# The shifted word of a float64 decoder moves from SBUF into idle columns of the attention's score banks, and h, y and the transposed tails share three PSUM buffers

## The chip, the cores and the metric

The program runs on one core of one Trainium2 chip. Its time is device microseconds from launch to end. The engines are named as in the profile: PE (TensorE, the matrix engine), PEld (its weight loads), DVE (VectorE), ACT (ScalarE), POOL (GpSimd) and SP (SyncE, which issues DMAs). Two kernels are held to differ when their times differ by more than about 0.2%.

## The reference, cut to what matters

Eight batches of eight heads, 576 positions, 64 columns per head; then a two-layer feed-forward network over all 4608 positions.

```python
scores = scale * q @ k.T                          # (8, 8, 576, 576)
thresh = max(scores, -1) - tau
scores = where(scores >= thresh, scores, -1e9)
attn = softmax(scores)
x = (attn @ v), heads side by side                # (4608, 512)
h = x @ w_in                                      # (512, 2048), w_in is float64
out = (h * tanh(softplus(h))) @ w_out             # (2048, 512), w_out is float64
```

The two weight matrices arrive as float64. The kernel turns them into float32 itself, from the two 32-bit words of each number: this is the decoding that the change edits.

## The kernel before

**Attention, and the first layer in its shadow.** The work is cut into 288 steps g. A step handles 128 query rows of a pair of heads; nine steps make a pair, 36 a batch. The scores of step g lie in one of two PSUM tiles, `s0` and `s1`, taken in turn (`smap[g % 2]`). Such a tile is two whole banks, 2 x 512 float32 columns a partition; the scores take 290 columns of the first bank and 286 of the second, a few columns at 508 hold a constant, and the rest is unused. In step g DVE takes the row maximum (`row_max`, "TENSOR_REDUCE st<-s" in the profile), ACT the exponential ("ACTIVATE e<-s,st"), DVE the mask with the row sum (`masked`, "SCALAR_TENSOR_TENSOR p<-s,st,e"), POOL the normalisation ("TENSOR_SCALAR p<-p,st"). One step later and more PE transposes p (tile `tp` for four blocks, `t5` for the tail block, shown as "t" in the profile, since numbers are left out of names), ACT rounds the transposed block to `hi`, DVE makes the rest `lo` (and `tk` for the tails), and PE multiplies them with v into `y`. From step 42 on PE also runs the first layer of the batch before (`gemm1`, matmuls into `h`), handed out in portions of a few matmuls per step (table `MIX`). ACT copies each finished h to `hst`, which goes to DRAM.

**Where the scores are issued.** `begin(g + 1)` issues the scores of the next step on PE. Up to step 41 it stands at the start of step g. From `LATE = 42` on it stands at the end of step g, in the middle of that step's portion of h matmuls. In both places it reuses the bank pair that step g - 1 read last, so its first matmul waits for `masked(g - 1)` on DVE.

**Decoding.** A piece is 128 x 256 numbers. ACT scales both words (`first`), DVE clamps the upper one from columns `a` to `b` (`clamp`, TENSOR_SCALAR on float32), shifts it from `b` back into `a` (`shift`, TENSOR_SCALAR on uint32), and merges the sign bit (`sign`, SCALAR_TENSOR_TENSOR on uint32, which reads `b` and `a`); POOL adds the lower word (`add`). All of it lies in SBUF (tile `dec`). There are 32 pieces of w_in, decoded in steps 3 to 55, then 16 pieces of half of w_out (`decode_w2`), one every 14 steps, and 16 pieces more that are decoded near the end of attention or later. For w_in, shift and sign follow each other in one step (`STAGES`, the first two entries); for `decode_w2` the sign comes two steps after the shift. In a step the shift is issued before `masked(g)`; the sign is issued before it up to step 38 and behind it from `JOIN = 39` on.

**PSUM.** There are eight banks. While attention runs: two for h and y in turn (pool `psh`), four for the scores, one for `tp`, one for `t5`. In the last batch's first layer, when attention is over, the banks of scores, tp and t5 have gone; three of h's five buffers are then in another pool (`psx`, "hx" in the profile), three are for the second layer.

**The second layer** follows, from about 980 us on: seven products per pair of token blocks (tiles x, y, z) over blocks of g = mish(h) read back from DRAM.

**What sets the order.** On PE, DVE, ACT and POOL the instructions run exactly in the order in which the Python code emits them (`InOrder`); each engine stops at the first instruction whose wait is not met. Waits are put in by the framework: an instruction that writes a tile waits for those that used it before, and a buffer that comes round waits for its last readers.

## Time and profile before

| | |
|---|---|
| median of 3 runs | 1331.6 us (1330.83 to 1331.86) |
| the profiled execution | 1333.22 us, of which the span of instructions is 1331.4 us |
| granted PE clock, mean | 0.997 |
| PE busy | 1296.8 us, 97% |
| PE weight loads | 1257.4 us, 94% |
| DVE busy | 1152.3 us, 87% |
| ACT busy | 1031.8 us, 77% |
| POOL busy | 750.0 us, 56% |

Nearly all instructions carry line 95 (the recording helper), so rows are told apart by operation and tiles. A row of the grouped view reads: line, engine, operation, out<-in, shape, count | busy time in all, mean ns of one | idle time of the engine before them and what ended it. A matmul's end is modelled, so two matmuls that follow each other overlap in the rows; the distance from start to start (about 0.13 us for an h matmul) is the pace. What an instruction of DVE takes contains the time in which it was held up after its start.

### The profile page before, as it was taken

To read this page: it belongs to the slowest core of one execution; us is meant where nothing else is said; L and a number is where in the kernel's file an instruction comes from. 1 tells how busy PE (TensorE), PEld (TensorE's weight loads), DVE (VectorE), ACT (ScalarE), POOL (GpSimd) and SP (SyncE) were. 2 spreads that over 40 slices of the span, in tenths; PEclk is the share of its full clock that TensorE was granted. 3 is DMA by queue.
4 is the path that set the end of the run, shared out by engine and by line. 5 is a ranking of instruction groups with operands and counts; after the bars stand their busy time and mean duration, and the time that the engine had idled before them with its cause. 6 is when DMAs were issued, how large, how long until landed. Compare 5 with 4: busy or idle time off the path is not lost.

```text
span 1331.4 us, 29917 instructions
## 1 busy us (share of the span) xinstructions
PE 1296.8 (97%) x9931; PEld 1257.4 (94%) x9931; DVE 1152.3 (87%) x2941; ACT 1031.8 (77%) x2320; POOL 750.0 (56%) x1080
## 2 busy tenths in 40 slices
PE   8997899999999999999999999999999999999998
PEld 7666889999999999999999999999999999999998
DVE  7999999999999999999999999997978666778764
ACT  6888788888888888888888888877767666557562
POOL 4879888788788887888878788774100000000000
PEclk9999999999999999999999999999999999999999
DMA  5333334333343343333433333324745454554430
GB/s 186 111 101 110 117 118 129 103 114 112 99 135 91 109 125 98 123 104 108 130 94 117 108 113 122 95 68 157 245 138 152 128 132 138 159 151 112 112 118 33
DMA packets 145930, 160.29 MB, mean 120 GB/s; under 512 B 34928, under 2 KB 128112, under 8 KB 145520
## 3 DMA queue, kind: packets, MB, share of 16 engines
q1 hardware_dynamic: 145776, 158.38, 39.1%
q8 instruction: 79, 1.29, 0.4%
q14 instruction: 75, 0.61, 0.2%
HBM read 109.05 MB, written 49.28 MB: 119 GB/s over the span
## 4 chain that ended last, share of the span: by engine, by line
PE 72%; DVE 13%; ACT 10%; issue 4%; POOL 0%; DVEq 0%; ACTq 0%; POOLq 0%
PE h L95 20%; PE y L95 16%; PE x L95 11%; PE s L95 8%; PE z L95 7%; PE tp L95 6%; DVE st L95 5%; ACT e L95 4%; DVE p L95 4%; PE hx L95 2%; DVE dec L95 2%; DVE lo L95 1%; ACT hi L95 1%; DVE tk L95 1%; ACT k L95 1%
## 5 line engine op out<-in xcount | busy, mean ns | idle before, releaser
L95 PE MATMUL h<-xh,w1h 128*128 128x288 f32 x952 | 288.0, 302 | 1.4 <-ACT yo L95 0.7
L95 PE MATMUL h<-xh,w1l 128*128 128x288 f32 x952 | 285.8, 300 | 0.0
L95 POOL TENSOR_SCALAR p<-p,st 128x576 f32<-128x576 f32 x288 | 244.5, 849 | 66.8 <-DVE st L95 44.2
L95 PE MATMUL h<-xl,w1h 128*128 128x288 f32 x952 | 281.3, 295 | 0.3 <-DVE xl L95 0.3
L95 ACT ACTIVATE e<-s,st 128x580 f32<-128x580 f32 x288 | 215.0, 747 | 62.9 <-DVE st L95 55.9
L95 DVE SCALAR_TENSOR_TENSOR p<-s,st,e 128x580 f32<-128x580 f32 x288 | 236.3, 820 | 19.3 <-ACT e L95 8.3
L95 PE MATMUL s<-k,q 128*128 128x286 f32 (+1 forms) x1280 | 231.2, 307 | 10.0 <-DVE p L95 9.6
L95 DVE TENSOR_REDUCE st<-s 128x1 f32<-128x580 f32 x288 | 217.9, 757 | 1.7 <-PE s L95 0.3
L95 PEld LDWEIGHTS s<-k,q 128*128 128x128 f32 x1280 | 189.0, 190 | 23.9 <-DVE p L95 21.0
L95 DVE TENSOR_TENSOR ring<-un,ring 128x512 fp32r<-128x512 f32 x252 | 157.0, 686 | 54.3 <-ACT ring L95 53.9
L95 DVE TENSOR_TENSOR lo<-tp,hi 128x512 fp32r<-128x512 f32 (+1 forms) x280 | 174.0, 630 | 27.6 <-ACT hi L95 23.6
L95 PE MATMUL tp<-ident,p 128*128 128x128 f32 x1152 | 174.1, 274 | 8.6 <-DVE lo L95 6.4
L95 PEld LDWEIGHTS h<-xh,w1h 128*128 128x128 f32 x952 | 179.9, 189 | 2.7 <-ACT yo L95 1.4
L95 ACT CAST hi<-tp 128x512 fp32r<-128x512 f32 (+1 forms) x280 | 149.8, 546 | 39.8 <-PE tp L95 35.3
L95 PEld LDWEIGHTS h<-xl,w1h 128*128 128x128 f32 x952 | 179.5, 189 | 0.5 <-DVE xl L95 0.5
L95 PEld LDWEIGHTS h<-xh,w1l 128*128 128x128 f32 x952 | 179.6, 189 | 0.0
L95 ACT CAST ring<-un 128x512 fp32r<-128x512 f32 x252 | 138.1, 618 | 32.4 <-DVE un L95 32.1
L95 PE MATMUL x<-ring,un 128*128 128x256 f32 x1296 | 156.4, 280 | 0.5 <-ACT ring L95 0.5
L95 PEld LDWEIGHTS tp<-ident,p 128*128 128x128 f32 x1152 | 139.3, 141 | 17.4 <-issue 6.4
L95 PEld LDWEIGHTS x<-ring,un 128*128 128x128 f32 x1296 | 153.9, 189 | 0.6 <-ACT ring L95 0.6
L95 PE MATMUL y<-hi,vs 128*128 128x256 f32 (+1 forms) x448 | 133.3, 320 | 8.0 <-ACT hst L95 6.9
L95 PE MATMUL y<-lo,vs 128*128 128x256 f32 (+1 forms) x448 | 122.7, 296 | 0.0
(78 smaller groups left out, 2537.4 us busy)
## 6 DMA issues: line engine op xcount, KB each, us to landing
hd<-hst SPq DMA_DIRECT2D x56, 576.0 KB, 3.4
r<-q SPq DMA_DIRECT2D x120, 160.0 KB, 2.3
r<-k SPq DMA_DIRECT2D x120, 160.0 KB, 2.3
out_t<-ost SPq DMA_DIRECT2D x36, 256.0 KB, 2.3
r<-v SPq DMA_DIRECT2D x56, 160.0 KB, 2.3
dec<-w_in SPq DMA_DIRECT2D x32, 256.0 KB, 2.9
un<-hd SPq DMA_DIRECT2D x16, 512.0 KB, 5.8
dec<-w_out SPq DMA_DIRECT2D x28, 256.0 KB, 2.8
```

The source lines that it names most:

```text
L95: made = method(*args, **kwargs)
```

## The change

The shifted word is no longer put into columns `a` of the SBUF tile. `shift` writes it as 2 x 128 columns, from column 320 on, into both banks of a score tile: that of the next step, `smap[1 - g % 2]`, with g the step in which the shift is issued (`turn`). `sign` reads it from there, wherever it comes later. This holds for all pieces of w_in, for the 16 of `decode_w2` and for 5 of the rest.

The pool `psh` gets three buffers in place of two, and the tail transposes `t5` take theirs from it, in turn with h and y, in place of a bank of their own. In the last batch's first layer three of five h tiles now come from `psh` and two from `psx`, where it was two and three.

```diff
-    def __init__(self, nc, st, hi, lo, to=None):
+    def __init__(self, nc, st, hi, lo, to=None, bits=None):
...
+        self.bits, self.t, self.tb = bits, self.a, self.b
...
     def shift(self):
-        self.nc.vector.tensor_scalar(self.a, self.b, 3, 0x7FFFFFF8, ALU.logical_shift_left, ALU.bitwise_and)
+        if self.bits:
+            self.t, self.tb = self.bits(), self.b.rearrange("p (a n) -> p a n", a=2)
+        self.nc.vector.tensor_scalar(self.t, self.tb, 3, 0x7FFFFFF8, ALU.logical_shift_left, ALU.bitwise_and)
...
     def sign(self):
-        self.nc.vector.scalar_tensor_tensor(self.b, self.b, 0x80000000, self.a, ALU.bitwise_and, ALU.bitwise_or)
+        self.nc.vector.scalar_tensor_tensor(self.tb, self.tb, 0x80000000, self.t, ALU.bitwise_and, ALU.bitwise_or)
...
-        psh = outer.enter_context(tc.tile_pool(name="psh", bufs=2, space=PSUM))
+        psh = outer.enter_context(tc.tile_pool(name="psh", bufs=3, space=PSUM))
...
-                smap, emap = [], []
+                smap, emap, turn = [], [], [0]
...
+                def bits():
+                    return smap[1 - turn[0] % 2][:, :, 320:320 + WC // 2].bitcast(U32)
...
-                    work = Decode(nc, home(), None, None, r12[:, f % 8])
+                    work = Decode(nc, home(), None, None, r12[:, f % 8], bits if n < 5 else None)
...
-                    work = Decode(nc, st, hi, lo)
+                    work = Decode(nc, st, hi, lo, None, bits)
...
-                    work = Decode(nc, st, None, None)
+                    work = Decode(nc, st, None, None, None, bits)
...
-                        t5 = pst.tile([P, P], F32, name="t5")
+                        t5 = psh.tile([P, P], F32, name="t5", tag="ph")
...
-                            if b < B - 1 or f % 5 < 2:
+                            if b < B - 1 or f % 5 < 3:
...
                 for g in range(NT + 5):
+                    turn[0] = g
...
-            psx = second.enter_context(tc.tile_pool(name="psx", bufs=3, space=PSUM))
+            psx = second.enter_context(tc.tile_pool(name="psx", bufs=2, space=PSUM))
```

The order of instructions on PE, DVE, ACT and POOL stays as it was up to the end of attention. What changes is what the instructions touch. The first place is DVE at the first piece of `decode_w2`, steps 62 to 65. In the rows `s0_121` and `s1_127` are the two score tiles, `dec_3299` the piece, `p` the masked probabilities, `st` small per-row numbers. The shift with its neighbours, before:

```order
L95 TENSOR_TENSOR lo_3527<-tp_3561,hi_3526 128x4x128
L95 TENSOR_TENSOR tk_3528<-t5_3566,tk_3528 64x128 x2
L95 TENSOR_SCALAR dec_3299<-dec_3299 128x256
L95 SCALAR_TENSOR_TENSOR p_3606,st_3582<-s0_121,st_3582,e0_122 128x580
L95 TENSOR_REDUCE st_3630<-s1_127 128x1
```

and of the change:

```order
L95 TENSOR_TENSOR lo_3527<-tp_3561,hi_3526 128x4x128
L95 TENSOR_TENSOR tk_3528<-t5_3566,tk_3528 64x128 x2
L95 TENSOR_SCALAR s1_127<-dec_3299 128x2x128
L95 SCALAR_TENSOR_TENSOR p_3606,st_3582<-s0_121,st_3582,e0_122 128x580
L95 TENSOR_REDUCE st_3630<-s1_127 128x1
```

The shift of step 62 now writes `s1`, which the scores of step 63 write next on PE. The sign, two steps later, before:

```order
L95 TENSOR_TENSOR lo_3627<-tp_3670,hi_3626 128x4x128
L95 TENSOR_TENSOR tk_3628<-t5_3675,tk_3628 64x128 x2
L95 SCALAR_TENSOR_TENSOR p_3709,st_3692<-s0_121,st_3692,e0_122 128x580
L95 SCALAR_TENSOR_TENSOR dec_3299<-dec_3299 128x256
L95 TENSOR_REDUCE st_3743<-s1_127 128x1
```

and of the change:

```order
L95 TENSOR_TENSOR lo_3627<-tp_3670,hi_3626 128x4x128
L95 TENSOR_TENSOR tk_3628<-t5_3675,tk_3628 64x128 x2
L95 SCALAR_TENSOR_TENSOR p_3709,st_3692<-s0_121,st_3692,e0_122 128x580
L95 SCALAR_TENSOR_TENSOR dec_3299<-dec_3299,s1_127 128x256
L95 TENSOR_REDUCE st_3743<-s1_127 128x1
```

The sign of step 64 stands behind that step's mask (`p_3709` from `s0`), reads `s1`, and the next use of `s1` on PE is the scores of step 65. In the built program the first matmul of those scores waits for the count of DVE's semaphore that this sign raises; before, it waited for the count that the mask of step 63 raises. The scores of step 63 wait in the same way for the shift of step 62, where they waited for the mask of step 61.

The second place is PE in step 64, where a tail transpose and a y follow each other (`t5_3675`, `y_3678`), with what they wait for at the end of a row. Before:

```order
L95 MATMUL tp_3670<-ident_80,p_3507 128x128 x3
L95 MATMUL t5_3675<-ident_80,p_3507 128x128
L95 MATMUL y_3678<-hi_3526,vs_3090 128x256 [waits Activation_49]
L95 MATMUL y_3678<-lo_3527,vs_3090 128x256
L95 MATMUL y_3678<-hi_3526,vs_3090 128x256
```

and of the change:

```order
L95 MATMUL t5_3675<-ident_80,p_3507 128x128 [waits Activation_49]
L95 MATMUL y_3678<-hi_3526,vs_3090 128x256 [waits Activation_49]
L95 MATMUL y_3678<-lo_3527,vs_3090 128x256
L95 MATMUL y_3678<-hi_3526,vs_3090 128x256
L95 MATMUL y_3678<-lo_3527,vs_3090 128x256
```

The order of the two is the same. The tail transpose now takes part in the round of h and y, and waits for ACT's copy out of the tile that had its buffer before it.

## The prediction

> **What bounds the kernel now.** I read the table of stages first: for each stretch its length, then busy time of PE, its weight loads, DVE, ACT and POOL, the granted clock and the DMA share.

> ```profile
> 0.00:131.00 131.00, 115.98 (x625) 90.55 (x626) 118.53 (x392) 103.05 (x259) 96.24 (x119) 0.99 0.43 127
> 131.00:190.00 59.00, 52.79 (x371) 50.08 (x371) 56.89 (x167) 46.70 (x120) 50.68 (x64) 0.96 0.41 127
> 190.00:900.00 710.00, 702.64 (x5389) 692.70 (x5388) 660.79 (x1923) 608.61 (x1471) 583.70 (x872) 1.00 0.35 109
> 940.00:1331.40 391.40, 386.41 (x3263) 386.04 (x3261) 283.98 (x382) 244.23 (x394) 1.08 (x1) 1.00 0.46 130
> ```

> There are two regimes. Up to 190 us, while w_in is decoded, DVE bounds (56.89 of 59.00 us between 131 and 190). From 190 on PE bounds: 702.64 of 710.00, so at most 7.4 us of its idle time can be won there, and whatever stops PE for longer comes on top. DVE has 49 us free in that stretch.

> The grouped view gives what the two edited instructions cost, sign (SCALAR_TENSOR_TENSOR) and shift (TENSOR_SCALAR); the two pairs are of 0 to 131 and of 190 to 900 us:

> ```profile
> L95 DVE SCALAR_TENSOR_TENSOR dec<-dec 128x256 uint32<-128x256 uint32 x24 | 17.9, 747 | 0.7
> L95 DVE TENSOR_SCALAR dec<-dec 128x256 uint32<-128x256 uint32 x24 | 8.9, 370 | 0.0
> ...
> L95 DVE SCALAR_TENSOR_TENSOR dec<-dec 128x256 uint32<-128x256 uint32 x16 | 11.3, 706 | 0.0
> L95 DVE TENSOR_SCALAR dec<-dec 128x256 uint32<-128x256 uint32 x16 | 5.9, 369 | 0.2
> ```

> How long they take undisturbed is in the view of the tile dec (minimum/median/maximum; its TENSOR_SCALAR row holds clamps and shifts alike):

> ```profile
> L95 DVE TENSOR_SCALAR dec<-dec x120: 272/295/2405, 20.9 to 938.1; 128x256 f32<-128x256 f32 x60, 128x256 uint32<-128x256 uint32 x60
> L95 DVE SCALAR_TENSOR_TENSOR dec<-dec x60: 414/528/2290, 23.8 to 938.9; 128x256 uint32<-128x256 uint32 x60
> ...
> L95 DVE TENSOR_TENSOR lo<-tp,hi 128x256 fp32r<-128x256 f32 x56 | 21.0, 417 | 6.2 <-ACT hi L95 5.6
> ```

> The sign loses 330 ns on average to something that holds it up, up to 2290 in all. The last row (grouped view) is the nearest relative of the new form: 256 columns, one operand in PSUM, one in SBUF, 417 ns.

> **The change part by part. Sign and shift.** The new sign should take about 420 ns, between 414 (undisturbed now) and 747 (if PSUM spares it nothing). No row shows a shift into PSUM: it lies between 272 (nothing changes) and 420; I take 410, since its operand no longer lies in SBUF alone, as with the 417 row. Up to 131 us each piece then gains 747 - 420 = 327 ns and loses 410 - 370 = 40, so 24 x 0.287 = 6.9 us on the engine that bounds. [...]

> Against the 6.9 us stands a wait. Up to step 41 the scores of step g + 1 are issued ahead of the shift of step g, into the tile that it writes, so the shift waits for them. Ends and starts, from the timeline:

> ```profile
> 22.96 1.14 PE L95 MATMUL s<-k,q 128*128 128x290 f32 x4
> 23.51 0.27 DVE L95 TENSOR_SCALAR dec<-dec 128x256 uint32<-128x256 uint32 x1
> ...
> 101.61 1.24 PE L95 MATMUL s<-k,q 128*128 128x290 f32 x4
> 102.53 0.82 DVE L95 TENSOR_SCALAR dec<-dec 128x256 uint32<-128x256 uint32 x1
> ```

> In the first the scores end at 24.10, 0.59 after the shift began; in the second 0.32 after. This is so at 10 of the 24 shifts, 4.7 us together. So this stretch wins about 2 us (between 6.9 won, if DVE absorbs the waits, and 3 lost, if the sign stays at 600 ns).

> **The scores behind the decoder, 190 to 900 us.** Here the scores of step g + 1 are in the middle of the h matmuls at the end of step g, and the built program makes them wait for the shift or the sign of step g. The first piece, from the timeline (start, duration):

> ```profile
> 205.40 0.70 PE L95 MATMUL s<-k,q 128*128 128x290 f32 x4
> 206.42 0.71 DVE L95 TENSOR_SCALAR dec<-dec 128x256 uint32<-128x256 uint32 x1
> ...
> 207.63 0.59 ACT L95 CAST hi<-tp 128x512 fp32r<-128x512 f32 x1 [0.73 <-PE tp L95]
> 208.96 0.67 DVE L95 TENSOR_TENSOR lo<-tp,hi 128x512 fp32r<-128x512 f32 x1
> ...
> 211.12 0.59 ACT L95 CAST hi<-tp 128x512 fp32r<-128x512 f32 x1
> 211.69 0.69 PE L95 MATMUL s<-k,q 128*128 128x290 f32 x4
> 211.75 0.69 DVE L95 TENSOR_TENSOR lo<-tp,hi 128x512 fp32r<-128x512 f32 x1
> 213.11 0.82 DVE L95 SCALAR_TENSOR_TENSOR p<-s,st,e 128x580 f32<-128x580 f32 x1
> 213.86 0.95 DVE L95 SCALAR_TENSOR_TENSOR dec<-dec 128x256 uint32<-128x256 uint32 x1
> ```

> Now the scores start at 205.40 and 211.69 without waiting. With the change the first must wait until the shift is done, 206.42 + 0.41 = 206.83, which is 1.43 us; the second until the sign is, 213.86 + 0.42 = 214.28, which is 2.59 us. Behind the waiting scores PE has the rest of its h matmuls, the transposes and y: nothing may pass. The last piece of the 16 reads the same:

> ```profile
> 859.36 0.70 PE L95 MATMUL s<-k,q 128*128 128x290 f32 x4
> 859.68 0.29 DVE L95 TENSOR_SCALAR dec<-dec 128x256 uint32<-128x256 uint32 x1
> ...
> 865.13 0.69 PE L95 MATMUL s<-k,q 128*128 128x290 f32 x4
> 866.44 0.91 DVE L95 SCALAR_TENSOR_TENSOR dec<-dec 128x256 uint32<-128x256 uint32 x1
> ```

> 0.73 and 1.73 us. Over all 16 the shifts give 19.5 us (mean 1.22), the signs 33.3 (mean 2.08), 52.7 together. To each of the 32 comes a restart, about 0.1 us (between 0.05, the usual gap from one engine's end to another's start, and the 0.2 of a weight load): 3 us. Does DVE catch up while PE stands? Only as far as it is behind. At 211.75 its `lo` starts 0.04 us after ACT's hi ended (211.12 + 0.59), so DVE follows PE's transposes there, and a late PE makes a late sign: no gain. At 208.96 it is behind by 0.74 (the hi of that step had ended at 207.63 + 0.59). I take the middle, 0.4 per piece, 7 us for 16. So this term is 52.7 + 3 - 7 = 49 us, bounded by 35 (each sign at 1.3 us, the smallest that occurs, and shifts at two thirds) and 56.

> [...]

> **131 to 190 us.** Eight signs of the last pieces of w_in have the same wait. First and last:

> ```profile
> 133.13 0.70 PE L95 MATMUL s<-k,q 128*128 128x290 f32 x4
> 135.27 2.29 DVE L95 SCALAR_TENSOR_TENSOR dec<-dec 128x256 uint32<-128x256 uint32 x1
> ...
> 174.60 0.56 PE L95 MATMUL s<-k,q 128*128 128x290 f32 x3
> 179.03 0.41 DVE L95 SCALAR_TENSOR_TENSOR dec<-dec 128x256 uint32<-128x256 uint32 x1
> ```

> 2.56 and 4.85 us, 20 us for the eight. But DVE bounds here, PE idles 6 us of the 59 anyway, and DVE gets shorter work (the next rows: 8 x (796 - 410 + 656 - 420) ns = 5 us).

> ```profile
> L95 DVE TENSOR_SCALAR dec<-dec 128x256 uint32<-128x256 uint32 x8 | 6.4, 796 | 0.0
> L95 DVE SCALAR_TENSOR_TENSOR dec<-dec 128x256 uint32<-128x256 uint32 x8 | 5.3, 656 | 0.0
> ...
> PE y L95 <- ACT hst L95: 4.9, 12, 0.8
> PEld y L95 <- ACT hst L95: 12.4, 27, 1.0
> ```

> I take 20 - 5 - 5 = 10 us, between 3 (DVE's wait for the 0.7 us of scores, eight times, less a part of its gain) and 20.

> **Three buffers.** The last two rows (waits, 190 to 900 us) are PE waiting to start a y until ACT has copied the h that held its buffer. Laid over this trace, y's first matmul follows that copy within 0.1 us at 59 places with two buffers, at 24 with three, since the tails now use the ring too. So 35/59 of the wait goes: 2.9 us by the matmul row, 7.4 by the row of weight loads, some more before 190 us. I take 6 won (3 to 9). The tails themselves wait nowhere: their buffer is free at least 1.0 us before. The last batch keeps five buffers for h: nothing, give or take 1.

> The sum against the execution profiled: 1333.2 - 2 + 49 + 10 - 6 = 1384. The median of the runs lies 1.6 below that execution: **1383 us**.

> **The rivals.** *The waits stand, but mostly hide.* For it: DVE has 49 us free between 190 and 900. Then after a shift's wait DVE would no longer be behind and the sign costs only what it does at best, 1.3 us, the shifts half: 16 x (1.3 + 0.6) = 30, and 131 to 190 costs 3: 1331.6 - 2 + 30 + 3 - 6 = 1357. Against it: DVE's 0.04 us at 211.75.

> *DVE's relief wins.* The excess of the signs over 420 ns is 7.9 us up to 131 us, and all of POOL's traffic with it gets smoother; with the buffers' 9 and 5 more up to 190, the time is 1331.6 - 7 - 5 - 9 = 1311. It decides from the point where the 32 waits cost under 21 us, 0.65 each; the rows above show 0.73 as one of the smallest.

> *The dense stretch locks.* From 131 to 190 us DVE waits for scores that wait for DVE, step by step, and its own loss comes on top of PE's 20; with no catching up later (56) and 4 for the buffers: 1331.6 + 25 + 56 - 4 = 1409.

> *The change does not do what it says:* the sign in PSUM stays at 700 ns. The first stretch then loses 5 us in place of winning 2, and each of 16 waits gets 0.28 longer: 1394. It goes with the forecast.

> **How the numbers follow.** Forecast with its neighbour, the slow sign: 0.75. Hiding: 0.12. Locked: 0.07. Relief: 0.04, no change 0.02. The range reaches from the hiding case to short of the locked one: 1355 to 1402. Faster by over 0.2% (2.7 us, what can be told from no change) 0.04, within 0.02, slower 0.94.

> **What would show it.** In the profile after: PE's scores wait for "DVE dec" and "DVE s" at some 40 places, 1 to 3 us each, and PE's busy share from 190 to 900 us falls from 99% to about 93%. The stretch is about 755 us long, with stops every 14 steps. Signs of about 420 ns everywhere, shifts of about 410. PE's waits of y for hst halve. It would be wrong if PE's scores showed no idle time before them after 190 us, or if the loss sat before 131 us or after 940.

## The result, and the profile after

The changed kernel takes 1395.4 us (median; 1393.6 to 1399.1), the kernel before 1331.7 (1330.8 to 1332.7). The ratio is 1.048, with a 95% interval from 1.0464 to 1.0498: the change costs 64 us. It lies inside the range of the prediction and 12 us above its value.

Where the time went shows best in windows that are cut at the same steps in both kernels (the row maxima of steps 42, 56 or 60, and 287 mark the cuts). Before, with the stretch, its length, then the busy time of PE, its weight loads, DVE, ACT and POOL, and the granted clock:

```profile
0.00:130.80 130.80, 115.78 (x624) 90.34 (x625) 118.33 (x392) 102.85 (x258) 96.04 (x119) 0.99 0.43 127
130.80:185.10 54.30, 48.09 (x335) 45.38 (x335) 52.43 (x156) 42.66 (x113) 46.43 (x58) 0.95 0.38 117
185.10:903.60 718.50, 711.14 (x5456) 701.20 (x5454) 668.94 (x1952) 615.57 (x1489) 590.57 (x883) 1.00 0.35 109
903.60:1331.40 427.80, 421.76 (x3523) 420.50 (x3521) 312.64 (x450) 270.72 (x463) 16.96 (x23) 1.00 0.47 137
```

and after:

```profile
0.00:128.80 128.80, 115.01 (x624) 90.57 (x625) 112.63 (x392) 102.85 (x258) 91.64 (x119) 0.98 0.43 129
128.80:196.80 68.00, 51.03 (x331) 49.27 (x331) 48.72 (x156) 43.12 (x111) 44.79 (x57) 0.89 0.31 93
196.80:965.80 769.00, 720.55 (x5461) 709.46 (x5459) 672.11 (x1952) 617.21 (x1490) 587.92 (x883) 0.99 0.33 102
965.80:1393.80 428.00, 421.71 (x3524) 420.50 (x3521) 312.68 (x450) 270.62 (x463) 16.83 (x23) 1.00 0.47 137
```

Up to step 42 the change wins 2.0 us. In the dense stretch that follows it loses 13.7, from step 56 to the end of attention 50.5, and behind that nothing. PE's busy share in the long stretch fell from 99.0% to 93.7%. PE's waits from 197 us on (engine and tile, what it waited for: total, times, longest):

```profile
PE s L95 <- DVE dec L95: 28.9, 16, 2.3
PE s L95 <- DVE s L95: 18.2, 16, 1.9
PE y L95 <- ACT hst L95: 0.9, 3, 0.5
```

These are the 32 waits of the forecast: the scores behind 16 signs ("DVE dec") and 16 shifts ("DVE s"), 47.1 us together. The timeline around the first sign of these 16; before the change, the same scores started at 211.69 us, without waiting:

```profile
225.27 0.29 PE L95 MATMUL h<-xl,w1h 128*128 128x288 f32 x1
...
226.37 0.82 DVE L95 SCALAR_TENSOR_TENSOR p<-s,st,e 128x580 f32<-128x580 f32 x1
227.12 0.41 DVE L95 SCALAR_TENSOR_TENSOR dec<-dec,s 128x256 uint32<-128x256 uint32 x1
227.59 0.81 PE L95 MATMUL s<-k,q 128*128 128x290 f32 x4 [2.02 <-DVE dec L95]
...
230.55 0.69 DVE L95 TENSOR_TENSOR lo<-tp,hi 128x512 fp32r<-128x512 f32 x1 [0.91 <-ACT hi L95]
```

PE has nothing to do from the last h matmul to 0.06 us after the sign. DVE then waits for the transposes that PE issues behind the scores (its `lo` stands 0.91 us for ACT's hi): it cannot use the stop to get ahead.

The two edited instructions take what they were expected to take, as the grouped view of the whole run shows (the sign before, then shift and sign after):

```profile
L95 DVE SCALAR_TENSOR_TENSOR dec<-dec 128x256 uint32<-128x256 uint32 x60 | 40.1, 668 | 1.1
...
L95 DVE TENSOR_SCALAR s<-dec 128x256 uint32<-128x256 uint32 x53 | 22.5, 424 | 3.7 <-PE s L95 3.1
L95 DVE SCALAR_TENSOR_TENSOR dec<-dec,s 128x256 uint32<-128x256 uint32 x53 | 22.1, 418 | 0.8
```

The sign is no longer held up (418 ns on average, where it was 668), the shift costs 424.

One thing was not forecast. PE's mean granted clock is 0.986, against 0.997. The clock's record shows stretches of 3.41 us at half the clock: two in the kernel before, both before 150 us, and eleven after the change, five of them between 197 and 966 us (each trace has one more at its very end). Each of those five begins within 1 us of the end of a stop of PE of 2.2 to 2.3 us. The four runs of the change differ in the same way: the fastest took 1393.6 us at a mean clock of 0.988, the slowest 1399.1 us at 0.984. One of the five, from the timeline and the windows:

```profile
364.91 0.80 PE L95 MATMUL s<-k,q 128*128 128x290 f32 x4 [2.25 <-DVE dec L95]
...
366.22 0.44 PE L95 MATMUL h<-xh,w1l 128*128 128x288 f32 x1
366.46 0.44 PE L95 MATMUL h<-xh,w1h 128*128 128x288 f32 x1
...
370.06 0.29 PE L95 MATMUL h<-xl,w1h 128*128 128x288 f32 x1
370.20 0.29 PE L95 MATMUL h<-xh,w1l 128*128 128x288 f32 x1
...
365.90:369.30 3.40, 3.40 (x17) 3.38 (x16) 1.43 (x5) 1.43 (x3) 1.51 (x2) 0.50 0.29 87
```

The h matmuls start 0.24 us apart in it, and 0.13 or 0.14 behind it. So such a stretch costs PE an estimated 1.3 to 1.7 us (17 matmuls where about 27 would have been done, by the 44 in 5.50 busy us just before; half of 3.41 at most). With it the long stretch adds up: 47.1 us of waits, 5 x 1.3 to 1.7 = 6.5 to 8.5 of half clock, less the 4.9 that the ring wins there (next section): 48.7 to 50.7, and 50.5 were measured.

### The profile page after: what moved, and what is told of

It reads as the page before. It is cut to its first block, busy times and chain, and to the rows that moved or that the text cites. A ratio compares the mean times of both kernels' runs of the same rounds, so it can differ in the third digit from the quotient of the medians.

```text
span 1393.8 us, 29940 instructions
## 1 busy us (share of the span) xinstructions
PE 1308.3 (94%) x9931; PEld 1269.8 (91%) x9931; DVE 1146.1 (82%) x2941; ACT 1033.8 (74%) x2320; POOL 741.2 (53%) x1080
## 4 chain that ended last, share of the span: by engine, by line
PE 76%; DVE 14%; ACT 5%; issue 4%; DMA 0%; DVEq 0%; SPq 0%; ACTq 0%
PE h L95 22%; PE y L95 15%; PE s L95 11%; PE x L95 11%; PE tp L95 7%; PE z L95 7%; DVE st L95 4%; DVE p L95 4%; DVE tk L95 2%; ACT e L95 2%; ACT hi L95 2%; DVE dec L95 2%; PE hx L95 1%; DVE s L95 1%; PE t L95 1%
## 5 line engine op out<-in xcount | busy, mean ns | idle before, releaser
L95 PE MATMUL s<-k,q 128*128 128x286 f32 (+1 forms) x1280 | 238.3, 314 | 72.9 <-DVE dec L95 43.4
L95 PE MATMUL h<-xh,w1h 128*128 128x288 f32 x976 | 297.3, 305 | 0.8 <-ACT xh L95 0.6
L95 PE MATMUL h<-xh,w1l 128*128 128x288 f32 x976 | 295.7, 303 | 0.0
L95 PE MATMUL h<-xl,w1h 128*128 128x288 f32 x976 | 291.5, 299 | 0.4 <-DVE xl L95 0.4
L95 POOL TENSOR_SCALAR p<-p,st 128x576 f32<-128x576 f32 x288 | 240.0, 833 | 81.9 <-DVE st L95 61.5
L95 PEld LDWEIGHTS s<-k,q 128*128 128x128 f32 x1280 | 190.7, 192 | 94.8 <-DVE dec L95 34.9
L95 DVE SCALAR_TENSOR_TENSOR p<-s,st,e 128x580 f32<-128x580 f32 x288 | 236.2, 820 | 15.4 <-ACT e L95 7.4
L95 DVE TENSOR_REDUCE st<-s 128x1 f32<-128x580 f32 x288 | 218.2, 758 | 34.1 <-PE s L95 22.6
L95 ACT ACTIVATE e<-s,st 128x580 f32<-128x580 f32 x288 | 215.2, 747 | 33.1 <-DVE st L95 27.7
L95 DVE TENSOR_TENSOR lo<-tp,hi 128x512 fp32r<-128x512 f32 (+1 forms) x280 | 175.0, 633 | 65.2 <-ACT hi L95 61.1
L95 ACT CAST hi<-tp 128x512 fp32r<-128x512 f32 (+1 forms) x280 | 149.7, 545 | 81.2 <-PE tp L95 76.7
L95 DVE TENSOR_TENSOR ring<-un,ring 128x512 fp32r<-128x512 f32 x252 | 156.8, 683 | 54.3 <-ACT ring L95 54.0
L95 PEld LDWEIGHTS h<-xh,w1h 128*128 128x128 f32 x976 | 186.7, 191 | 1.9 <-ACT yo L95 0.9
L95 PEld LDWEIGHTS h<-xl,w1h 128*128 128x128 f32 x976 | 187.0, 192 | 0.6 <-DVE xl L95 0.6
L95 PEld LDWEIGHTS h<-xh,w1l 128*128 128x128 f32 x976 | 187.0, 192 | 0.0
L95 PE MATMUL tp<-ident,p 128*128 128x128 f32 x1152 | 176.8, 277 | 3.8 <-DVE lo L95 2.2
L95 ACT CAST ring<-un 128x512 fp32r<-128x512 f32 x252 | 138.1, 618 | 32.5 <-DVE un L95 31.9
L95 ACT COPY hst<-h 128x288 f32<-128x288 f32 x244 | 96.0, 401 | 85.8 <-PE h L95 83.2
L95 PE MATMUL x<-ring,un 128*128 128x256 f32 x1296 | 156.4, 280 | 0.3 <-DVE ost L95 0.3
L95 PEld LDWEIGHTS x<-ring,un 128*128 128x128 f32 x1296 | 153.9, 189 | 0.5 <-ACT ring L95 0.5
L95 PEld LDWEIGHTS tp<-ident,p 128*128 128x128 f32 x1152 | 142.7, 143 | 10.8 <-POOL k L95 2.8
L95 POOL TENSOR_TENSOR x<-x,yo 64x256 f32<-64x256 f32 (+1 forms) x111 | 88.7, 799 | 89.1 <-ACT yo L95 84.6
```

The costliest lines, as they stand in the source:

```text
L95: made = method(*args, **kwargs)
```

## The experiments

The theory: the scores' wait for the decoder is the loss; the ring of three PSUM buffers and the undisturbed sign win a little; the half clock behind long stops adds the rest. The rivals: the ring of h, y and tails costs; PSUM operands cost wherever they lie; the stops alone cost, without the clock.

### The buffers alone

The shifted word stays in SBUF for all pieces; the ring of three remains.

```diff
-                    work = Decode(nc, home(), None, None, r12[:, f % 8], bits if n < 5 else None)
+                    work = Decode(nc, home(), None, None, r12[:, f % 8])
...
-                    work = Decode(nc, st, hi, lo, None, bits)
+                    work = Decode(nc, st, hi, lo)
...
-                    work = Decode(nc, st, None, None, None, bits)
+                    work = Decode(nc, st, None, None)
```

> Three PSUM buffers for y, h and tails, while the shifted word stays in SBUF. Theory (the loss of the change is the scores' wait for the decoder, the ring of three wins a little): 1326 us, between 1323 and 1329; PE's wait of y for hst falls from 6.9 us to 3 or less. Rival (the tails in the ring of h and y are what costs): 1340 us or more, with PE waits before t or h.

1325.5 us (1325.1 to 1328.3), 0.9952 of the kernel before (0.994 to 0.9965): 6.6 us won. Its profile is level with the kernel before at step 60 and 4.9 us ahead at step 287. PE's waits and those of its weight loads, from 190 to 900 us:

```profile
PE y L95 <- ACT hst L95: 1.8, 5, 0.7
...
PEld y L95 <- ACT hst L95: 4.1, 9, 1.0
```

They were 4.9 and 12.4 before. The rival that the ring costs time falls.

### The word in the score tiles alone

Two buffers for h and y and a bank for the tails, as before; the shifted word as in the change.

```diff
-        psh = outer.enter_context(tc.tile_pool(name="psh", bufs=3, space=PSUM))
+        psh = outer.enter_context(tc.tile_pool(name="psh", bufs=2, space=PSUM))
...
-                        t5 = psh.tile([P, P], F32, name="t5", tag="ph")
+                        t5 = pst.tile([P, P], F32, name="t5")
...
```

> The shifted word in the score tiles as in the change, with two buffers for h and y and a bank for the tails, as before. Theory: all of the loss, plus the ring's gain undone: 1400 us, between 1396 and 1405. Rival (the ring takes part in the loss): under 1385 us.

1400.6 us, ratio 1.051 (1.0497 to 1.0532). All of the loss is in this part, and the ring takes 5.2 us off it.

### Without the pieces of w_out

```diff
-                    work = Decode(nc, st, None, None, None, bits)
+                    work = Decode(nc, st, None, None)
```

> The change, but the 16 pieces of decode_w2 (one every 14 steps) keep the shifted word in SBUF; the 32 pieces of w_in have it in the score tiles. Theory: the 50 us that the change loses between steps 60 and 287 go, and the ring's 4 us come to light: 1341 us, of which about 14 are lost between steps 42 and 56. Rival (PSUM operands as such, or the ring, cost time everywhere): 1370 us or more.

1339.9 us, ratio 1.005 (1.0034 to 1.0065). Its profile is 12.5 us behind at step 60 and 7.5 behind at the end: the loss of the dense stretch, less the ring's 5. The 16 pieces of w_out are worth 55 us, though they are under a third of the 53 pieces that the change touches.

### One column in place of the word

The kernel before, word in SBUF. Behind shift and sign of the 16 pieces of w_out DVE writes one column of the score tile.

```diff
+                def touch():
+                    nc.vector.memset(smap[1 - turn[0] % 2][:, 0, 320:321], 0.0)
...
     def shift(self):
         self.nc.vector.tensor_scalar(self.a, self.b, 3, 0x7FFFFFF8, ALU.logical_shift_left, ALU.bitwise_and)
+        self.touch()
...
     def sign(self):
         self.nc.vector.scalar_tensor_tensor(self.b, self.b, 0x80000000, self.a, ALU.bitwise_and, ALU.bitwise_or)
+        self.touch()
...
-                    work = Decode(nc, st, None, None)
+                    work = Decode(nc, st, None, None, None, touch)
```

> The kernel before, where the word stays in SBUF; behind the shift and behind the sign of the 16 pieces of decode_w2, DVE writes one unused column of the score tile that the change would use (32 memsets, 0.06 us each). Theory (it is the wait on the tile that costs, not the decoding): about as much as the change loses from step 60 on, with the ring's gain undone: 1385 us, between 1375 and 1392. Rival (what costs is where the operands lie): 1333 us.

1400.5 us, ratio 1.052 (1.0499 to 1.0533). 32 memsets of 59 ns (1.9 us in all) cost 68 us. That the wait costs, and not where the operands lie, is shown. My number was 15 us too low, and the time lies outside the range that I gave. Waits from 197 us on, and the sign in that window:

```profile
PE s L95 <- DVE s L95: 54.3, 32, 3.0
...
L95 DVE SCALAR_TENSOR_TENSOR dec<-dec 128x256 uint32<-128x256 uint32 x16 | 13.1, 820 | 0.0
```

The sign in SBUF is held up (820 ns), which makes the stops longer, up to 3.0 us, and eleven stretches of half clock follow them in place of five (mean clock 0.984): 54.3 + 11 x 1.3 to 1.7 = 69 to 73, against 69.5 measured between steps 60 and 287.

### The sign ahead of the mask

```diff
-JOIN = 39
+JOIN = 400
...
-                        if len(work) == 3 and g >= JOIN:
+                        if len(work) == 3 and g >= min(JOIN, NT):
```

> The change, with the sign ahead of the mask in every step (JOIN out of reach). The wait of the scores for the sign gets shorter by one mask, 0.85 us, at 24 places: 20 us less, and some stops of PE that lowered its clock get too short for it. Theory: 1370 us, between 1360 and 1380. Rival (the place in DVE's order does not matter): 1395 us.

1368.7 us, ratio 1.027 (1.0254 to 1.0285): 27 us less by nothing but the sign's place in DVE's order. Waits from 197 us on:

```profile
PE s L95 <- DVE s L95: 18.3, 16, 1.9
PE s L95 <- DVE dec L95: 16.7, 16, 1.5
```

The waits for signs fell from 28.9 to 16.7, 0.76 each, about a mask (0.82); those for shifts stayed. No stop there was longer than 1.9 us, and the clock stayed full from 197 us to the end of attention (1.00 between 208 and 966 us). From step 56 to 287 the profile gains 20 us on that of the change: 12.2 by the waits, and the other 7.7 is about what five stretches of half clock cost.

### Stops filled with idle transposes

In the change, ahead of the scores that wait for a piece of w_out, PE transposes the identity into the tp bank, 6 times for a shift and 10 for a sign; nothing reads them.

```diff
...
+        self.near.append(6)
         self.nc.vector.tensor_scalar(self.t, self.tb, 3, 0x7FFFFFF8, ALU.logical_shift_left, ALU.bitwise_and)
...
     def sign(self):
+        self.near.append(10)
...
                     turn[0] = g
+                    near.clear()
...
+                            if near:
+                                fill = pst.tile([P, 4, P], F32, name="tp")
+                                for _ in range(max(near)):
+                                    nc.tensor.transpose(fill[:, 0, :], ident, ident)
                             begin(g + 1)
```

> The change, with transposes of the identity into the tp bank ahead of the waiting scores of decode_w2 pieces: 6 where they wait for a shift, 10 where for a sign, about 0.1 us each, nothing reads them. They add some 260 transposes, 26 us of PE work, and shorten nothing. Theory with the clock (after a stop PE runs at half clock for 7.3 us at times, 5 times between steps 60 and 287, up to 3.6 us each): the stops are broken up, the clock stays, 1383 us, between 1376 and 1390, mean clock 0.99 or more. Rival (the stops alone cost): 1395 us or more, with the clock as it was or no effect of it.

1388.3 us (1386.9 to 1388.4), ratio 1.042 (1.0401 to 1.0432), 7.1 us under the change with 256 matmuls more on the engine that bounds. (The stretch of half clock is 3.41 us long, not 7.3 as I had written, so it is worth half of what stands there.) Waits from 197 us on, with the row of the mean clock:

```profile
PE tp L95 <- DVE lo L95: 7.4, 17, 0.8
PE s L95 <- DVE dec L95: 6.7, 15, 0.7
PE s L95 <- DVE s L95: 2.2, 10, 0.3
...
core 0: 1386.5 us, clock 0.994
```

No stop is over 0.8 us any more (the fill itself waits for the tp bank), and the five stretches of half clock are gone (clock 1.00 between 208 and 966 us). The work added shortens nothing by itself, so the rival that the stops alone cost, without the clock, falls; 7.1 us for five stretches is 1.4 each. The forecast of 1383 was 5 us too low; it had put up to 3.6 us on each stretch.

### Two versions without the wait

First, the word in the score tiles up to step 41 only:

```diff
                 def bits():
+                    if turn[0] >= LATE:
+                        return None
```

> The change, but the shifted word is in the score tiles only up to step 41, where the sign stands ahead of the mask; from step 42 on it stays in SBUF. Theory: no scores wait for the decoder any more: 1326 of the buffers alone, less 2 us won up to step 42, 1324 us. Rival (every piece costs): 1335 us or more.

1323.8 us (1323.6 to 1325.0), ratio 0.9938 (0.9925 to 0.995). Second, from step 42 on shift and sign both behind the mask of step g, in the tile that this mask has just read:

```diff
     def join(self):
+        if self.held:
+            self.shift(True)
         self.sign()
...
-                    return smap[1 - turn[0] % 2][:, :, 320:320 + WC // 2].bitcast(U32)
+                    if turn[0] >= LATE and not held:
+                        return None
+                    return smap[turn[0] % 2 if held else 1 - turn[0] % 2][:, :, 320:320 + WC // 2].bitcast(U32)
```

> The change, but from step 42 on shift and sign both stand behind the mask of step g, and use the tile that this mask has just read, which is written next by the scores of step g + 2, a step later. Theory: the scores of step g + 1 wait for the mask of g - 1 again, no new wait of PE; DVE keeps its undisturbed signs (5 us less of work between 131 and 190 us, where it bounds): 1320 us, between 1316 and 1326. Rival (a word in PSUM costs wherever it lies): over 1340 us.

1324.7 us (1323.7 to 1324.9), ratio 0.994 (0.9927 to 0.9952). PE's waits for signs in the whole run, then the edited instructions up to 131 us:

```profile
PE s L95 <- DVE dec L95: 0.6, 2, 0.4
...
L95 DVE TENSOR_SCALAR s<-dec 128x256 uint32<-128x256 uint32 x24 | 10.1, 422 | 3.2 <-PE s L95 3.1
L95 DVE SCALAR_TENSOR_TENSOR dec<-dec,s 128x256 uint32<-128x256 uint32 x24 | 10.1, 419 | 0.7
```

With the word in the same columns, and no row of PE's scores waiting for a shift, the wait is down to 0.6 us, since the next writer of that tile comes a step later. So the rival that PSUM operands cost time wherever they lie falls as well. Both versions beat both kernels by more than their intervals, mostly through the ring: over the buffers alone they win 1.7 and 0.9 us, which their intervals do not separate. The 5 us that I expected between steps 42 and 56 from undisturbed signs did not come: at step 56 both profiles are 3.1 us ahead of the kernel before, with and without them. Why a shorter DVE does not help there I did not settle.

## Why the prediction was right, and where it was short

**The bound and the place of the loss** held: nothing before 131 us, nothing behind attention, and the scores' stops behind signs and shifts in between.

**Up to step 41**, 2 us won: 2.0 measured. The shift's waits for scores came to 3.1 us in place of 4.7; the sign takes 419 ns (747 before, 771 with the buffers alone), the shift 422 (370 before). For 24 pieces these sizes give 7.9 - 1.3 - 3.1 = 3.5 us, so that the 2 was met is in part luck; why no more than 2.0 came is not settled.

**190 to 900 us**, 49 us: the waits are 47.1, of which the shifts 18.2 (19.5 without restart and catching up) and the signs 28.9 (33.3). What I took off for DVE's catching up was about right, and the 0.04 us at 211.75 had said rightly that it catches up no further there.

**131 to 190 us**, 10 us: 13.7 measured. PE waited 14.5 us for signs there, 7 times, and 2.4 once for a k; the clock was 0.89 in the stretch, 0.95 before. How much of the 3.7 us too little belongs to each was not separated.

**Three buffers**, 6 us won: 6.6 by themselves, 5.2 beside the waits. The wait of y for hst fell further than by 35/59.

**The term that was missing** is the clock. The sum priced a stop at its own length. Some stops of 2.2 us and more also halved PE's clock for 3.41 us: some 7 us in the long stretch, and perhaps a part of the 4 that the dense stretch ran over. Of the 12 us between forecast and result, the long stretch holds 7.5 (43 forecast with the buffers, 50.5 measured) and the dense one 3.7. The row of the stages held a hint: the clock of 0.96 between 131 and 190 us, where PE already had a stop of 2.28 us, at 137 us.

**The rivals.** Hiding fell by the 47.1 us. Relief fell: its decision point was 0.65 us per wait, and 1.47 was measured; POOL's busy time up to step 42 did fall, from 96.04 to 91.64 us. The slow sign fell (418 ns in place of 700), though its 1394 us is the number nearest to the result: it would have got there for another reason. The locked stretch was the direction in which the forecast was short, but only by 4 us of the 15 that it asked for there.

## What to carry to other kernels

Columns of a PSUM tile that nobody reads are free in space, not in time: whoever writes them becomes a predecessor of the tile's next writer (here 32 memsets of one such column cost 68 us). Before a scratch value is put into a buffer that another engine refills, look up which instruction the refill waits for now, and where the new writer stands behind it in its engine's order. Here one place earlier in DVE's order was worth 27 us, and the other tile of the pair, behind the mask, 71. And a stop of the bounding engine is to be priced with what follows it, its clock included (here an estimated 1.3 to 1.7 us more behind five of them).

## What the runs showed of the hardware that I had not expected

A second thing: work that nobody needs made the kernel 7.1 us faster, because it kept PE from stopping long enough to lose its clock. With the idle transposes no stop of PE from 197 us to the end of attention was over 0.8 us, where the change has nine over 2.0, and the granted clock was 1.00 between 208 and 966 us, where the change has 0.99.
